# Splitting the matmuls of an accumulated output into two of half the columns, in a channel-attention and feed-forward kernel

## The chip, the cores and the metric

The kernel runs on one core of a Trainium2 chip. The metric is the device time of one execution in microseconds (us), the median of several runs.

## What is computed

Two batches of 6016 tokens with 256 channels go through an attention over channels, and the result through a feed-forward layer with 2048 hidden units. The reference, cut:

```python
def _attn_ref(q, k, v, tau):               # B, N, C = 2, 6016, 256
    qn = q / (np.linalg.norm(q, axis=1, keepdims=True) + 1e-06)
    kn = k / (np.linalg.norm(k, axis=1, keepdims=True) + 1e-06)
    s = kn.transpose(0, 2, 1) @ qn / tau
    ...
    return (v @ a).astype(np.float32)      # a: softmax of s

def _moe_ref(x, w_in, w_out):              # 12032 tokens, 256 -> 2048 -> 256
    h = x @ w_in
    g = h * (1.0 / (1.0 + np.exp(-h)))
    return (g @ w_out).astype(np.float32)
```

## The kernel before, in words

The first part (about 121 us) loads q and k, forms the 256 x 256 scores of the first batch on TensorE in float32 (L244), turns them into the attention matrix, and decodes the two weight matrices. `mix` (L361) multiplies the attention into w_in, so that what is left is two large products: w_in mixed with the attention, by v; and w_out, by the activated hidden units.

The tokens go by in 12 "pairs" (L386): five of 1024 tokens and one of 896 for each batch. A pair is two halves of `h` tokens, h = 512 or 448, and `h` is the number of columns of every large matmul. For each pair there are eight steps `i`, one for each 256 hidden units. `emit_pair_group` (L499) makes the hidden units of one step in seven products of a Strassen-Winograd scheme (`product`, L507), each of three float16 matmuls (L509) that add up in a PSUM bank; ScalarE and VectorE copy, add and apply SiLU (L516, L521, L525), and `finish` splits each tile of 128 hidden units by `h` tokens into a float16 high and low part, `hl` (`split`, L123 on ScalarE and L124 on VectorE).

`emit_out` (L467) takes one such tile and adds its share to the output: for each of the two blocks `e` of 128 output channels, three matmuls (L480) of `h` columns, of w_out's low part by hl's high part, high by low, and high by high. They add up in a PSUM bank `o` over all 16 tiles (NF) of one half of a pair, so a bank gets 48 matmuls. Every matmul has a weight load of its own before it. When the count `c` reaches 16, ScalarE (L489) and VectorE (L493) scale the two banks into `sb`, and SP's queue writes it out (L497).

The order of TensorE's work is that of the program text: `emit_pair_group` yields four times a step, and at each yield at most one pending tile (two in parts of the first pair) goes through `emit_out`; background work (the next pair's v, the second batch's attention) is queued behind markers. TensorE executes its instructions in order, but for weight loads, which are drawn ahead of matmuls.

Of the kernel before, what the change touches and what calls it, by code (L numbers as in the profile page):

```python
# [16 lines left out]
P = 128  # L17
#: Operands of the large products are scaled by powers of two to at most 2**TOP.
TOP = 13
#: The hidden activations are scaled down by 2**-GS: 256 products of at most 2**(2 * TOP).  # L20
GS = 2 * TOP + 8 - 15
# [3 lines left out]
def channel_attention_then_silu_ffn(ctx, tc, q, k, qT, kT, vT, tau, w_in, w_out, outT):  # L25
# [34 lines left out]
    def small_psum(name):  # L60
        """Before the first output accumulates, its banks are free."""
        if early[0]:
            return ps_o.tile([P, 512], F32, tag="o", name=name)
        return ps_b.tile([P, 512], F32, tag="z", name=name)

    @contextmanager
    def at(priority):
        """Instructions of lower number go first where several could."""
        was = tc.cur_priority
        tc.cur_priority = priority  # L70
        yield
        tc.cur_priority = was

    def pow2_scale(amax, tag, bufs=1):
        """amax: largest magnitude by partition. Returns (s, 1/s): a power of two with
        |x| s < 2**TOP. Yields where TensorE waits for VectorE."""
        pt = small_psum("pt")
        nc.tensor.transpose(pt[:1, :P], amax, ident)
        mx = sm.tile([1, 1], F32, tag="mx", name="mx")
        nc.vector.tensor_reduce(out=mx, in_=pt[:1, :P], op=ALU.max, axis=AX.X)  # L80
        yield
        pb = small_psum("pb")
        nc.tensor.matmul(pb[:, :1], ones[:1, :], mx, start=True, stop=True)
        bound = sm.tile([P, 1], F32, tag="bound", name="bound")
        nc.vector.tensor_scalar(
            out=bound, in0=pb[:, :1], scalar1=2.0**-40, scalar2=2.0**40, op0=ALU.max, op1=ALU.min
        )
        yield
        floor2 = sm.tile([P, 1], F32, tag="floor2", name="floor2")
        nc.vector.tensor_scalar(  # L90
            out=floor2.bitcast(U32), in0=bound.bitcast(U32), scalar1=0x7F800000, scalar2=None,
            op0=ALU.bitwise_and,
        )
        inv = sm.tile([P, 1], F32, tag=f"i{tag}", name=f"i{tag}", bufs=bufs)
        nc.vector.tensor_scalar(
            out=inv, in0=floor2, scalar1=2.0 ** (1 - TOP), scalar2=None, op0=ALU.mult
        )
        s = sm.tile([P, 1], F32, tag=f"s{tag}", name=f"s{tag}", bufs=bufs)
        nc.vector.reciprocal(s, inv)
        yield  # L100
        return s, inv

    def amax_of(parts, tag):
        """Largest magnitude by partition over the tiles."""
        m = sm.tile([P, len(parts)], F32, tag=tag, name=tag)
        for i, x in enumerate(parts):
            nc.vector.tensor_reduce(
                out=m[:, i : i + 1], in_=x, op=ALU.max, axis=AX.XY if len(x.shape) == 3 else AX.X,
                apply_absolute_value=True,
            )  # L110
            yield
        r = sm.tile([P, 1], F32, tag=f"{tag}1", name=f"{tag}1")
        nc.vector.tensor_reduce(out=r, in_=m, op=ALU.max, axis=AX.X)
        yield
        return r

    def split(src, hi, lo, s=None):
        """hi + lo = src * s."""
        if s is None:
# [14 lines left out]
    def decode(dst, raw, top=None):  # L134
        """dst <- float32 of the float64 in raw (as 64 raw bits). Yields after each step.
        top: takes the largest high word by partition, without sign."""
        k, n = raw.shape[1:]
        w = raw.bitcast(U32).rearrange("p k (n two) -> p k n two", two=2)
        low, high = w[:, :, :, 0], w[:, :, :, 1]
        t = hp.tile([P, k, n], U32, tag="g", name="t", bufs=6)  # L140
        # What float32 has no exponent for becomes 0.
        nc.scalar.activation(out=t.bitcast(F32), in_=high.bitcast(F32), func=AF.Abs)
# [29 lines left out]
    def warm(func, x):  # L172
        """Has func's table loaded while ScalarE waits."""
        nc.scalar.activation(out=junk, in_=x, func=func)

    # -- channel attention ---------------------------------------------------------------
    # Tokens that come at a time; the first ones sooner.
    edges = [0, *range(2, J, G), J], [*range(0, J, G), J]
# [18 lines left out]
    def square_sums():  # L197
        """Squares of the last batch's q and k, summed along the tokens. Yields."""
        edges = list(range(0, N, NT)) + [N]
# [15 lines left out]
    def attention(b, ahead):  # L215
        """Yields after each piece of TensorE's work."""
        if b == 0:
# [32 lines left out]
        while b and "go" not in norms:  # L250
            yield
        # Squared norms by partition.
        tot = sm.tile([P, 2 * KC], F32, tag="tot", name="tot", bufs=1)
# [21 lines left out]
        yield  # L275
        # One step of Heron's rule makes the root exact to float32.
        rn = sm.tile([P, 2 * KC], F32, tag="rn", name="rn", bufs=1)
# [56 lines left out]
        yield  # L334
        # The softmax's denominators scale the rows of a's product with w_in.
        rows = sm.tile([P, KC], F32, tag="rows", name="rows")
# [10 lines left out]

    # Left operands of the seven products of Strassen and Winograd. Rows 1 and 2 of the pair's
    # product are its odd and its even block of hidden units.
    A21, A11, A22, A12, S1, S2, S3, S4 = range(8)  # L350
    # Right operands. The columns are the halves of the tokens.
    B11, T1, B21, B22, T2, T3, T4 = range(7)
    mixed = {}

    def mix(b, i):
        """w_in's hidden units of pair i, mixed by the attention, in parts."""
        aT, rows = mixer[b]
# [26 lines left out]

    # -- tokens --------------------------------------------------------------------------
    pairs = [(b, n, min(NT, N - n)) for b in range(B) for n in range(0, N, NT)]  # L386
# [57 lines left out]
    def back_of(p):  # L444
        """What takes the accumulated output of pair p back to its scale."""
        back = sm.tile([P, 1], F32, tag="back", name="back")
        nc.vector.reciprocal(back, parts[p][2])
        nc.vector.tensor_scalar(
            out=back, in0=back, scalar1=weights["out"][1], scalar2=None, op0=ALU.mult
        )  # L450
        return back
# [6 lines left out]
    def finish(t):  # L458
        """hi and lo of a tile of hidden activations."""
        h = t["h"]  # L460
# [6 lines left out]
    def emit_out(t):  # L467
# [6 lines left out]
        for e in range(KC):  # L474
# [4 lines left out]
            for i, (a, m) in enumerate(((wo_lo, 0), (wo_hi, 1), (wo_hi, 0))):  # L479
                nc.tensor.matmul(  # L480
                    o[:, :h], a[:, f, ee], hl[:, m, :h],
                    start=(c == 1 and i == 0), stop=(c == NF and i == 2),
                )
        if c == NF:
# [14 lines left out]
    def emit_pair_group(p, i):  # L499
        """Hidden units of pair i for the tokens of pair p. Yields where other work of TensorE  # L500
        may stand, four times."""
        b, n, w = pairs[p]
# [55 lines left out]
    def steps(gen):  # L558
        """Runs gen to its end; its value."""
        while True:  # L560
            try:
                next(gen)
            except StopIteration as e:
                return e.value
# [14 lines left out]
    def prepare_out():  # L579
        """w_out in parts; its raw halves stand where later tokens will."""  # L580
        halves = [vp.tile([P, NI, C], F32, tag="v", name="wo", bufs=3) for _ in range(2)]
# [29 lines left out]
    def high_to_f32(x):  # L611
        """In place: from the high word of positive float64 to float32, its mantissa cut."""
        t = sm.tile([P, 1], U32, tag="hw", name="hw", bufs=1)
# [40 lines left out]

    # Priorities, by phase.
    VALUES, RAW, CHAIN, DECODE, MAIN = 20000, 15000, 10000, 25000, 100000
    # The groups of tokens behind which w_in's parts are loaded.
    RAW_AT = (4, 5, 6, 7, 8, 9, 9, 9)

    with at(0):  # L660
# [3 lines left out]
        nc.vector.reciprocal(rtau, tau_sb)  # L664
        # Both norms come doubled.
        nc.vector.tensor_scalar(out=rtau, in0=rtau, scalar1=4.0, scalar2=None, op0=ALU.mult)
# [21 lines left out]
    def mark():  # L688
        """What background() traces next goes behind what was traced by now."""
        found = {}  # L690
# [4 lines left out]
    def background(gen, n=1):  # L695
        """Next steps of gen, issued no sooner than what mark() saw last."""
        start = len(traced())
# [54 lines left out]
    def prepare():  # L752
        """Next steps of w_out's preparation, and of the other batch's attention."""
        nonlocal filler
# [100 lines left out]
```

## Time and profile before

| | |
|---|---|
| three runs | 1067.05, 1069.79, 1070.09 us; median 1069.79 us |
| span of the profiled execution, first to last instruction | 1063.3 us (its own time isn't given beside it) |
| TensorE matmuls | 1040.3 us, 98% of the span, 4886 |
| TensorE weight loads | 523.7 us, 49%, 4886 |
| VectorE | 728.5 us, 69% |
| ScalarE | 837.3 us, 79% |
| mean granted TensorE clock | 1.000 |

Between the span and the median of the runs lie 6.5 us. Busy time is the union of an engine's records. A matmul's record (379 ns for 512 columns) is longer than the distance to the next one, because matmuls are pipelined: what a matmul costs is read from the distance of starts, not from its mean duration.

### The profile page before, as it was taken

Reading aid. Unit: us, or ns where it says so; the run is one execution under the profiler, and the core shown is the slowest. Engines: PE = TensorE matmul, PEld = TensorE weight load, DVE = VectorE, ACT = ScalarE, POOL = GpSimd, SP = SyncE. Lnnn points to the kernel's source line nnn. Section 1 sums busy time; section 2 is a strip of 40 time slices with the busy share of each in tenths; the row PEclk is TensorE's granted clock in tenths of the full one; section 3 lists DMA queues with packets and bytes.
Section 4 is the critical chain, followed back from the end, with each engine's and each line's share of the span. In section 5 each row is a group of like instructions: output and inputs, shape, how many; then the busy total and the mean of one; then the engine's idle time right before and its main releaser. Section 6 shows DMA issues by size and latency. Waiting matters only on the chain.

```text
span 1063.3 us, 13048 instructions
## 1 busy us (share of the span) xinstructions
PE 1040.3 (98%) x4886; PEld 523.7 (49%) x4886; DVE 728.5 (69%) x1288; ACT 837.3 (79%) x1371; POOL 0.7 (0%) x6
## 2 busy tenths in 40 slices
PE   7889999999999999999999999999999999999998
PEld 6667544444444444444555544444444444444554
DVE  6989669657657657667768767657657657656654
ACT  5657568889989989988878878878878878878875
POOL 0000000000000000000000000000000000000000
PEclk9999999999999999999999999999999999999999
DMA  8978711111412400200200200200200100100100
GB/s 317 343 261 288 270 42 40 60 60 58 133 39 60 137 1 1 80 0 1 80 1 1 75 1 1 79 1 1 75 1 1 40 1 1 40 1 1 40 1 35
DMA packets 25391, 70.83 MB, mean 67 GB/s; under 512 B 2544, under 2 KB 3824, under 8 KB 25328
## 3 DMA queue, kind: packets, MB, share of 16 engines
q1 hardware_dynamic: 25328, 70.00, 18.9%
q8 instruction: 38, 0.62, 0.2%
q14 instruction: 25, 0.20, 0.1%
HBM read 57.67 MB, written 12.32 MB: 66 GB/s over the span
## 4 chain that ended last, share of the span: by engine, by line
PE 81%; ACT 8%; DVE 6%; DMA 4%; issue 1%; SPq 0%; DVEq 0%
PE o L480 40%; PE x L509 20%; PE y L509 10%; PE z L509 5%; PE sc L244 3%; ACT g L525 2%; ACT hl L123 2%; PE w L361 2%; DMA q_t<-in_q 2%; DVE g L521 1%; ACT c L516 1%; DVE hl L124 1%; DMA raw<-in_w_out 1%; DMA held<-in_w_in 1%; DMA raw<-in_w_in 1%
## 5 line engine op out<-in xcount | busy, mean ns | idle before, releaser
L480 PE MATMUL o<-hl,wo_hi 128*128 128x512 f16 (+1 forms) x1536 | 450.5, 375 | 0.0
L124 DVE SCALAR_TENSOR_TENSOR hl<-g,sg,hl 128x512 f16<-128x512 f32 (+1 forms) x384 | 282.5, 739 | 175.1 <-ACT hl L123 173.5
L509 PEld LDWEIGHTS <-W 128*128 128x128 f16 x2016 | 196.1, 98 | 228.4 <-issue 5.7
L509 PE MATMUL x<-m,W 128*128 128x512 f16 (+1 forms) x1152 | 306.4, 374 | 1.5 <-DVE g L521 0.9
L525 ACT ACTIVATE g<-g,alpha 128x512 f32<-128x512 f32 (+1 forms) x288 | 203.7, 707 | 117.0 <-DVE g L521 115.5
L480 PE MATMUL o<-hl,wo_lo 128*128 128x512 f16 (+1 forms) x768 | 287.5, 375 | 0.0
L123 ACT ACTIVATE hl<-g,sg 128x512 f16<-128x512 f32 (+1 forms) x384 | 271.5, 711 | 10.1
L480 PEld LDWEIGHTS <-wo_hi 128*128 128x128 f16 x1536 | 150.3, 98 | 173.4
L509 PE MATMUL y<-m,W 128*128 128x512 f16 (+1 forms) x576 | 153.2, 375 | 0.0
L516 ACT COPY c<-x 128x512 f32<-128x512 f32 (+1 forms) x192 | 110.5, 576 | 25.1 <-PE x L509 22.4
L480 PEld LDWEIGHTS <-wo_lo 128*128 128x128 f16 x768 | 75.1, 98 | 86.9
L244 PE MATMUL sc<-q_t,k_t 128*128 128x256 f32 x376 | 88.2, 387 | 13.5 <-DMA q_t<-in_q 13.3
L521 DVE TENSOR_TENSOR g<-z,c 128x512 f32<-128x512 f32 (+1 forms) x96 | 65.2, 680 | 40.8 <-PE z L509 33.8
L521 DVE TENSOR_TENSOR g<-x,c 128x512 f32<-128x512 f32 (+1 forms) x96 | 65.2, 679 | 40.9 <-PE x L509 40.6
L244 PEld LDWEIGHTS sc<-q_t,k_t 128*128 128x128 f32 x376 | 71.1, 193 | 27.3 <-issue 9.4
L521 DVE TENSOR_TENSOR g<-y,c 128x512 f32<-128x512 f32 (+1 forms) x96 | 65.0, 677 | 26.3 <-ACT c L516 25.4
L509 PE MATMUL z<-m,W 128*128 128x512 f16 (+1 forms) x288 | 76.5, 375 | 0.0
L516 ACT COPY c<-y 128x512 f32<-128x512 f32 (+1 forms) x96 | 54.7, 570 | 11.9 <-PE y L509 10.7
L525 ACT ACTIVATE g<-x,alpha 128x512 f32<-128x512 f32 (+1 forms) x96 | 63.4, 660 | 0.8 <-PE x L509 0.8
L124 DVE SCALAR_TENSOR_TENSOR m<-v_t,sv,m 128x512 f16<-128x512 f32 (+1 forms) x48 | 35.0, 735 | 0.1
L123 ACT ACTIVATE m<-v_t,sv 128x512 f16<-128x512 f32 (+1 forms) x48 | 33.7, 708 | 0.0
L124 DVE SCALAR_TENSOR_TENSOR m<-x,sv,m 128x512 f16<-128x512 f32 (+1 forms) x36 | 26.4, 737 | 9.3 <-ACT m L123 9.3
(111 smaller groups left out, 467.3 us busy)
## 6 DMA issues: line engine op xcount, KB each, us to landing
k_t<-in_k SPq DMA_DIRECT2D x22, 512.0 KB, 5.8
q_t<-in_q SPq DMA_DIRECT2D x22, 512.0 KB, 5.9
v_t<-in_vT SPq DMA_DIRECT2D x10, 1024.0 KB, 5.1
outT<-sb SPq DMA_DIRECT2D x40, 256.0 KB, 2.0
turned<-in_qT SPq DMA_DIRECT2D x10, 512.0 KB, 4.4
turned<-in_kT SPq DMA_DIRECT2D x10, 512.0 KB, 3.5
raw<-in_w_out SPq DMA_DIRECT2D x8, 512.0 KB, 4.3
raw<-in_w_in SPq DMA_DIRECT2D x5, 512.0 KB, 6.9
```

Of the source, the lines that this page charges most:

```text
L123: nc.scalar.activation(out=hi, in_=src, func=AF.Copy, scale=s)
L124: nc.vector.scalar_tensor_tensor(out=lo, in0=src, scalar=s, in1=hi, op0=ALU.mult, op1=ALU.subtract)
L244: nc.tensor.matmul(sc[:, cb, :], t["k"][:, i, cb * P : (cb + 1) * P], t["q"][:, i, :], start=(j + i == 0 and cb == 0), stop=(j + i == J - ...
L361: nc.tensor.matmul(w[:, cb * C : (cb + 1) * C], aT[:, db, cb * P : (cb + 1) * P], w_in_sb[:, db, i * C : (i + 1) * C], start=(cb + db == 0 ...
L480: nc.tensor.matmul(o[:, :h], a[:, f, ee], hl[:, m, :h], start=(c == 1 and i == 0), stop=(c == NF and i == 2),)
L509: nc.tensor.matmul(bank[:, :h], wm[:, u, a - 1], m[:, y, x, :h], start=(first and j == 0), stop=(j == 2), skip_group_check=True,)
L516: nc.scalar.copy(t[:, :h], bank[:, :h])
L521: nc.vector.tensor_tensor(out=g[:, :h], in0=bank[:, :h], in1=t[:, :h], op=ALU.add)
L525: nc.scalar.activation(out=g[:, :h], in_=src[:, :h], func=AF.Silu, scale=alpha)
```

## The change

In `emit_out`, each of the three matmuls of a block is issued as two, over the first and the second half of the columns (256 and 256, or 224 and 224), both with the same left operand, so that each has a weight load apiece. The start flag, which marks a bank as to be overwritten, is kept for the first half of the first matmul alone; the second half of the bank is overwritten too, since nothing has been written there since. The rest of the diff takes comments and docstrings out, lines for lines, and changes nothing that is executed.

```diff
             for i, (a, m) in enumerate(((wo_lo, 0), (wo_hi, 1), (wo_hi, 0))):
-                nc.tensor.matmul(
-                    o[:, :h], a[:, f, ee], hl[:, m, :h],
-                    start=(c == 1 and i == 0), stop=(c == NF and i == 2),
-                )
+                for u in range(0, h, h // 2):
+                    nc.tensor.matmul(
+                        o[:, u : u + h // 2], a[:, f, ee], hl[:, m, u : u + h // 2],
+                        start=(c == 1 and i == 0 and u == 0), stop=(c == NF and i == 2),
+                        skip_group_check=True,
+                    )
```

## Rows read from the trace of the kernel before

**Rows 1.** The page's first two parts: busy time, share of the span and instructions of each engine; the granted TensorE clock in 40 slices, in tenths, 9 being 90% or more.

```profile
PE 1040.3 (98%) x4886; PEld 523.7 (49%) x4886; DVE 728.5 (69%) x1288; ACT 837.3 (79%) x1371; POOL 0.7 (0%) x6
...
PEclk9999999999999999999999999999999999999999
```

**Rows 2.** The page's fourth part: the chain of work that ended last, shares of the span by engine, then by line.

```profile
PE 81%; ACT 8%; DVE 6%; DMA 4%; issue 1%; SPq 0%; DVEq 0%
PE o L480 40%; PE x L509 20%; PE y L509 10%; PE z L509 5%; PE sc L244 3%; ACT g L525 2%; ACT hl L123 2%; PE w L361 2%; DMA q_t<-in_q 2%; DVE g L521 1%; ACT c L516 1%; DVE hl L124 1%; DMA raw<-in_w_out 1%; DMA held<-in_w_in 1%; DMA raw<-in_w_in 1%
```

**Rows 3.** Busy time by windows: the stretch, its length, then for each engine busy us and (x) the count, the granted clock, the DMA share and GB/s.

```profile
121.00:200.00 79.00, 78.25 (x357) 38.30 (x356) 61.29 (x120) 60.54 (x105) 0.00 (x0) 1.00 0.21 73
200.00:440.00 240.00, 240.00 (x1115) 109.06 (x1114) 159.34 (x258) 212.95 (x347) 0.00 (x0) 1.00 0.20 65
440.00:600.00 160.00, 158.86 (x781) 81.35 (x779) 113.06 (x217) 132.88 (x228) 0.00 (x0) 1.00 0.08 27
600.00:1000.00 400.00, 400.00 (x1864) 182.86 (x1862) 267.51 (x433) 318.26 (x503) 0.00 (x0) 1.00 0.06 21
1000.00:1063.30 63.30, 58.66 (x311) 30.14 (x308) 31.72 (x49) 44.93 (x74) 0.00 (x0) 0.99 0.04 15
```

**Rows 4.** Groups of instructions with shapes kept apart: the matmuls of L480 (count, busy us, mean ns of a record).

```profile
L480 PE MATMUL o<-hl,wo_hi 128*128 128x512 f16 x1280 | 381.2, 379 | 0.0
...
L480 PE MATMUL o<-hl,wo_lo 128*128 128x512 f16 x640 | 242.4, 379 | 0.0
L480 PE MATMUL o<-hl,wo_hi 128*128 128x448 f16 x256 | 69.3, 352 | 0.0
...
L480 PE MATMUL o<-hl,wo_lo 128*128 128x448 f16 x128 | 45.1, 352 | 0.0
```

**Rows 5.** Two stretches without a pause, TensorE alone, by windows (length, busy us, count, clock, DMA share, GB/s): in the first every matmul has 512 columns, in the second 448. Each window begins inside the record of the first counted matmul and ends just before the next one after the last counted starts.

```profile
640.53:679.85 39.32, 39.32 (x183) 1.00 0.08 27
1000.45:1049.41 48.96, 48.96 (x260) 1.00 0.00 1
```

**Rows 6.** The timeline of TensorE's matmuls (start us, us): the first matmul counted in the first stretch of rows 5 and the one that follows its last, then the same of the second stretch (the first of the two that the row merges).

```profile
640.36 0.38 PE L480 MATMUL o<-hl,wo_lo 128*128 128x512 f16 x1
...
679.86 0.38 PE L509 MATMUL x<-m,W 128*128 128x512 f16 x1
...
1000.24 0.54 PE L480 MATMUL o<-hl,wo_hi 128*128 128x448 f16 x2
...
1049.42 0.35 PE L480 MATMUL o<-hl,wo_lo 128*128 128x448 f16 x1
```

**Rows 7.** The line L480 by itself: duration of its weight loads and matmuls, minimum/median/maximum in ns, with the forms.

```profile
L480 PEld LDWEIGHTS <-wo_hi x1536: 96/98/100, 121.4 to 1058.1; 128*128 128x128 f16 x192
...
L480 PEld LDWEIGHTS <-wo_lo x768: 96/98/98, 121.2 to 1057.7; 128*128 128x128 f16 x192
```

**Rows 8.** The chain of work in order of time: start us, us, what. Two pieces in which TensorE's stream itself is the chain.

```profile
121.54 1.29 PE o L480 x6
122.84 1.73 PE w L361 x8
```

**Rows 9.** The timeline around 63.3 us: three matmuls of 128 float32 columns in a row (two of L323, one of L78), the one after them, and their weight loads.

```profile
63.27 0.38 PE L323 MATMUL tp<-ident,e 128*128 128x128 f32 x2
63.48 0.27 PE L78 MATMUL pt<-ident,wtop 128*1 128x128 f32 x1
63.59 0.38 PE L244 MATMUL sc<-q_t,k_t 128*128 128x256 f32 x1
...
63.17 0.24 PEld L323 LDWEIGHTS tp<-ident,e 128*128 128x128 f32 x2
63.38 0.08 PEld L78 LDWEIGHTS pt<-ident,wtop 128*1 128x1 f32 x1
```

**Rows 10.** The timeline around 448 us, seen through narrow windows: the last three of four matmuls of 128 float32 columns (L291), the L480 matmul after them, and that one's weight load with the last of L291's before it.

```profile
447.88 0.50 PE L291 MATMUL rq_ps<-diag,ones 128*128 128x128 f32 x3
448.00 0.19 PEld L291 LDWEIGHTS rq_ps<-diag,ones 128*128 128x128 f32 x1
448.11 0.10 PEld L480 LDWEIGHTS <-wo_hi 128*128 128x128 f16 x1
...
448.22 0.38 PE L480 MATMUL o<-hl,wo_hi 128*128 128x512 f16 x1
```

**Rows 11.** The timeline around 949.6 us, seen through two narrow windows: the weight loads of L509 after a pause, first one, then the first two together.

```profile
949.59 0.10 PEld L509 LDWEIGHTS <-W 128*128 128x128 f16 x1
...
949.59 0.11 PEld L509 LDWEIGHTS <-W 128*128 128x128 f16 x2
```

**Rows 12.** The timeline around 20.9 us, where TensorE's sequencer had nothing queued: a weight load after a wait, and the matmul behind it; [idle before it, and what ended that].

```profile
20.84 0.08 PEld L78 LDWEIGHTS pt<-ident,av 128*1 128x1 f32 x1 [1.01 <-issue]
20.87 0.27 PE L78 MATMUL pt<-ident,av 128*1 128x128 f32 x1 [0.64 <-DVE av L113]
```

**Rows 13.** DMA queues, kind: packets, MB, share of 16 engines; the queue of instruction fetches that goes with TensorE's count.

```profile
q8 instruction: 38, 0.62, 0.2%
```

**Rows 14.** Waits of TensorE from 121 us on: who waited for whom, us in total, times, longest us.

```profile
PEld L509 <- issue: 5.1, 16, 0.9
PEld pb L83 <- DVE g L521: 3.8, 9, 0.4
...
PE x L509 <- DVE g L521: 0.9, 2, 0.6
```

## The prediction

> **What bounds the kernel now.** I read the page's busy times first, then the chain, then the busy times by stage. TensorE is busy for 98% of the span and its granted clock is full, the 2.4 GHz level, in all slices [rows 1]. That alone proves little, since a matmul's record is longer than the time it takes in a stream. The chain says more: 81% of it is TensorE, and half of that is the line that the change splits, L480 [rows 2]. By stage it is plainer still: from 200 to 440 us and from 600 to 1000 us TensorE shows no idle time at all, in 440 to 600 us 1.1 us, in 121 to 200 us 0.8 us, and the 4.6 us of the last window are the way of the last output to memory [rows 3]. ScalarE is the next engine, at 89% of the stretch from 200 to 440 us (212.95 of 240) and at 80% of the one from 600 to 1000 us. So what TensorE's stream gains or loses behind 121 us arrives at the end nearly one for one. L480 has no part in the first 121 us.
>
> **What one matmul of the stream costs.** Its distance to the next one, which two stretches without a pause give, one for each width. With 512 columns: 183 matmuls in 679.86 - 640.36 = 39.50 us, 215.8 ns each. With 448: 260 in 1049.42 - 1000.24 = 49.18 us, 189.2 ns [rows 5, 6]. 64 columns are worth 26.7 ns, 0.417 ns a column, one cycle at 2.4 GHz. At that price 512 columns take 213.3 ns and 448 take 186.7, so 2.5 ns of each distance belong to the matmul whatever its width. Each of these matmuls had a weight load of its own, so a load is in the price already.
>
> **The change, part by part.**
>
> Matmuls: L480 has 1280 + 640 of 512 columns and 256 + 128 of 448, 2304 in all [rows 4]. Each becomes two, with the same columns in sum. Columns cost what they did; the fixed part comes once more: 2304 x 2.5 ns = 5.8 us. By the stream's price a half of 256 columns takes 106.7 + 2.5 = 109.2 ns.
>
> Weight loads: 2304 more. One takes 98 ns by its record [rows 7], and today it lies beside a matmul of 216 ns. Is 109 ns cover enough? The trace has no matmul of 256 float16 columns, so I bound it by two nearby cases of about 107 ns of streaming (128 float32 columns; eight records of 256 float32 columns take 1.73 us in the stream, 216 ns each, six of 512 float16 columns 1.29, 215 ns: a float32 column costs two cycles) [rows 8]. Around 63.3 us three such matmuls, each behind a load, start at 63.27 and end their turn at 63.59: 107 ns each [rows 9]. Around 448 us three start at 447.88 and the next one of L480 at 448.22: 113 ns each, with loads of 190 ns, and the last of the three distances had a 100 ns load of L480 in it [rows 10]. The low end is thus nothing beyond the fixed part, the high end 113 - 109.2 = 3.8 ns for each of 4608 halves, 17.5 us more. I take the low end, because what stretches the second case is the length of a float32 load: after a pause two float16 loads follow each other within some 10 to 20 ns (the record of one is 0.10 us, of two together 0.11) [rows 11], so nearly all of the 98 ns is latency that overlaps.
>
> Issue: twice as many instructions for the same time, two each 109 ns. Where the sequencer had nothing queued, a matmul follows its load after 30 ns (20.84, 20.87) [rows 12]: 60 ns for a pair, under 109. Code: 38 fetches brought some 9,800 instructions of TensorE, 16 KB each [rows 13]; 4608 more instructions need 18 more fetches, against stretches of 240 and 400 us in which the present ones left no idle time [rows 3]. Taken as nothing; without that cover a fetch would have to show as a pause, and none does.
>
> What hides a little of it: TensorE waits now and then for a tile from VectorE or ScalarE, in all 1.9 us of plain idle time from 121 to 600 us [rows 3], with the waits of single loads listed one by one [rows 14]. A longer stretch of L480 ahead of such a wait shortens it. At most these 1.9 us come back, at least none; I take 0.6 us, a third, since most waits for L83 hang on TensorE's own earlier work. No wait, DMA or buffer is added: a bank's readers come after its last matmul, as before. ScalarE and VectorE get 0.5% more time for the same work.
>
> Sum: 5.8 - 0.6 = +5.2 us. On the profiled execution that is a span of 1063.3 + 5.2 = 1068.5 us; the 6.5 us between span and median stay. 1069.8 + 5.2 = 1075.0 us, 0.5% slower. A measurement of this kernel can tell about 0.3%, 3.2 us, from no change.
>
> **The rivals.**
>
> Not slower. The fixed 2.5 ns belong to the exchange of one set of weights for another, not to a matmul; the second half brings the set that is there already (or its load is dropped), follows without a gap, and the sum is 0, or -0.6 with the shorter waits: 1069 to 1070 us. It decides if the second half starts 106.7 ns behind the first and not 109. Against it: the price is the same wherever it can be read, behind 98 ns loads and behind one of 84 ns with a single column [rows 9]. For it: no row shows the same weights twice in a row. To be faster by 3.2 us it would also have to remove more idle time than the 1.9 us there are.
>
> Loads that don't fit. Halves at 113 ns, as around 448 us [rows 10]: 5.8 + 17.5 = 23.3 us, 1093 us; in part, at 111 ns, some 14 us, 1084 us. Against it, the 10 to 20 ns between two loads [rows 11].
>
> Issue-bound. If an instruction in a long stream took the sequencer twice the 30 ns, 60 ns, a pair would take 120 ns: 4608 x 10.8 = 50 us more, 1126 us. Against it, the two instructions 30 ns apart with nothing queued ahead of them [rows 12]. The Trainium skill's page "TensorE: Matmul & The Clock Gate" (Part 1, "Wait — 56ns, not 53.3ns?") allows for this case: it puts a matmul at about 62 ns where the sequencer's firmware decodes it, which with as much for a load would make 1144 us. The trace disagrees, with half of that for an instruction.
>
> Serial loads. If a load could not lie beside a matmul that uses the whole array, 2304 more would cost 98 ns each, 226 us: 1301 us. The same page says so (Part 3, "What overlaps and what doesn't": loads overlap matmuls in flight only in other row groups). The trace disagrees: 216 ns a matmul leave no room for a serial 98 ns beside 213 ns of columns [rows 5, 7].
>
> **How the numbers follow.** Chances: the forecast 0.74; not slower 0.10; loads that don't fit 0.12; issue-bound 0.03; serial loads 0.01. The likeliest gives 1075.0 us. The range: low end 1070.0, which is the "not slower" case at its top, and also the forecast if the runs land as low as the fastest one shown (1067.05) with part of the waits returned; high end 1089, between the partly and the wholly exposed load. Left out are most of the issue-bound and serial cases, the far end of the loads, and the lower half of "not slower": about 0.15 together. Slower by over 0.3%: 0.66 of the forecast's 0.74 (the rest falls within, by scatter) + 0.12 + 0.03 + 0.01 = 0.82. Within 0.3%: 0.08 + 0.07 = 0.15. Faster: 0.03.
>
> **What would show it.** 7190 matmuls and as many loads, 4608 on L480; L480's halves 109 ns apart and the 224-column ones 96; a block that was six matmuls, 1.29 us [rows 8], at 1.31; no pause of TensorE where a fetch lands. Halves 111 to 113 ns apart show the load, 120 the sequencer, 106.7 within a pair the "not slower" case. I am wrong if the order of TensorE's instructions around L480 has changed, or if idle time appears where there is none now.

## The result, and the profile after

The changed kernel took 1073.80 us, the median of 12 runs (1071.62 to 1079.82); the kernel before 1066.55 us, the median of 12 (1064.80 to 1070.09). The ratio is 1.0071, 95% interval 1.0054 to 1.0089: slower by 7.6 us, 5.8 to 9.5. The forecast was slower by 5.2 us, just below that interval.

The page of the changed kernel: busy time, share and count of each engine; the granted clock in tenths; the queue of instruction fetches; the chain that ended last, by line. They answer to [rows 1, 2, 13].

```profile
PE 1046.6 (98%) x7190; PEld 746.8 (70%) x7190; DVE 730.2 (68%) x1288; ACT 840.1 (79%) x1371; POOL 0.7 (0%) x6
...
PEclk9999999999999999999999999999999999999999
...
q8 instruction: 56, 0.92, 0.3%
...
PE o L481 41%; PE x L511 20%; PE y L511 11%; PE z L511 5%; PE sc L244 3%; DMA q_t<-in_q 2%; ACT g L527 2%; PE w L361 2%; ACT hl L123 1%; DMA k_t<-in_k 1%; DVE g L523 1%; ACT c L518 1%; DVE hl L124 1%; ACT m L123 1%; DMA raw<-in_w_out 1%; DMA held<-in_w_in 1%
```

7190 matmuls and loads, 18 more fetches, as counted ahead. (L480 is L481 now, and the lines of the products and adds are two further down.) What one tile (two blocks `e`) costs stands in the chain of work in order of time (start us, us, what), from a stretch without a pause:

```profile
642.16 1.31 PE o L481 x12
643.47 0.65 PE x L511 x3
```

Twelve halves in 1.31 us are 109.2 ns each, where six whole matmuls took 1.29 us [rows 8]: the halves cost the 2.5 ns apiece and nothing else. 2304 x 2.5 ns = 5.8 us, and 1.8 us of the difference are still to be found. Busy time by windows, with the columns of [rows 3] and to be held against them:

```profile
121.00:200.00 79.00, 78.02 (x524) 54.28 (x523) 60.81 (x120) 59.97 (x103) 0.00 (x0) 1.00 0.20 67
200.00:440.00 240.00, 240.00 (x1696) 165.67 (x1694) 159.51 (x258) 211.80 (x343) 0.00 (x0) 1.00 0.20 65
440.00:600.00 160.00, 157.63 (x1145) 115.09 (x1144) 110.79 (x214) 132.56 (x227) 0.00 (x0) 1.00 0.08 27
600.00:1000.00 400.00, 400.00 (x2824) 277.35 (x2822) 266.72 (x431) 317.60 (x500) 0.00 (x0) 1.00 0.05 19
```

TensorE's plain idle time from 440 to 600 us is 2.4 us, and was 1.1; from 121 to 200 us it is 1.0, and was 0.8. It is idle for longer than before, though VectorE and ScalarE, whose tiles it waits for, have the same work and slightly more time for it.

Whole runs of one kernel spread by 5 to 8 us, more than what is sought, so I read the traces over the main stretch: from the start of the first matmul of the output to the end of the last one, each from its row in the timeline (start us, us). For the changed kernel 1065.34 - 120.26 = 945.08 us:

```profile
120.26 0.38 PE L481 MATMUL o<-hl,wo_lo 128*128 128x256 f16 x2
...
1064.79 0.55 PE L481 MATMUL o<-hl,wo_hi 128*128 128x224 f16 x4
```

Beside it I give TensorE's waits in that stretch. Each matmul's start is held against the median distance behind matmuls of the same width and type (216, 189, 109, 96 ns and so on); where it comes over 10 ns later, what is over the median counts, summed over the stretch.

### The profile page after: what moved, and what is told of

Read it like the earlier page. It is cut to its first block, busy times and chain, and to the rows that moved or that the text cites. A ratio compares the mean times of both kernels' runs of the same rounds, so it can differ in the third digit from the quotient of the medians.

```text
span 1069.9 us, 17658 instructions
## 1 busy us (share of the span) xinstructions
PE 1046.6 (98%) x7190; PEld 746.8 (70%) x7190; DVE 730.2 (68%) x1288; ACT 840.1 (79%) x1371; POOL 0.7 (0%) x6
## 4 chain that ended last, share of the span: by engine, by line
PE 82%; ACT 7%; DVE 5%; DMA 5%; issue 1%; SPq 0%; DVEq 0%; ACTq 0%
PE o L481 41%; PE x L511 20%; PE y L511 11%; PE z L511 5%; PE sc L244 3%; DMA q_t<-in_q 2%; ACT g L527 2%; PE w L361 2%; ACT hl L123 1%; DMA k_t<-in_k 1%; DVE g L523 1%; ACT c L518 1%; DVE hl L124 1%; ACT m L123 1%; DMA raw<-in_w_out 1%; DMA held<-in_w_in 1%
## 5 line engine op out<-in xcount | busy, mean ns | idle before, releaser
L481 PE MATMUL o<-hl,wo_hi 128*128 128x256 f16 (+1 forms) x3072 | 455.5, 270 | 0.0
L481 PEld LDWEIGHTS <-wo_hi 128*128 128x128 f16 x3072 | 299.8, 98 | 30.5
L481 PE MATMUL o<-hl,wo_lo 128*128 128x256 f16 (+1 forms) x1536 | 290.1, 270 | 0.0
L481 PEld LDWEIGHTS <-wo_lo 128*128 128x128 f16 x1536 | 150.1, 98 | 91.0
```

The costliest lines, as they stand in the source:

```text
L481: nc.tensor.matmul(o[:, u : u + h // 2], a[:, f, ee], hl[:, m, u : u + h // 2], start=(c == 1 and i == 0 and u == 0), stop=(c == NF and i ...
```

## The experiments

All main stretches and waits, worked out as above from one trace each (two each of the kernel before and the changed one show how well they repeat):

| kernel | main stretch, us | against before | TensorE's waits, us | stretch less waits, us | ratio of times (95%) |
|---|---|---|---|---|---|
| before (first trace, again) | 937.28, 937.48 | 0 | 6.4, 6.5 | 930.9, 931.0 | again: 1.0001 (0.9987 to 1.0015) |
| changed (first trace, again) | 945.08, 944.92 | +7.7, +7.5 | 8.4, 8.2 | 936.7, 936.7 | 1.0071 (1.0054 to 1.0089), 1.0064 (1.0044 to 1.0083) |
| split, old order | 942.26 | +4.9 | 5.6 | 936.7 | 1.0060 (1.0040 to 1.0079) |
| new order, no split | 940.91 | +3.5 | 10.0 | 930.9 | 1.0031 (1.0020 to 1.0043) |
| new order of TensorE alone | 938.59 | +1.2 | 7.7 | 930.9 | 1.0003 (0.9983 to 1.0024) |
| new order of ScalarE and VectorE alone | 940.05 | +2.7 | 9.2 | 930.9 | 1.0019 (1.0007 to 1.0031) |
| split, halves outermost, old order | 942.37 | +5.0 | 5.7 | 936.7 | 1.0060 (1.0035 to 1.0084) |
| quarters, old order | 953.32 | +15.9 | 5.1 | 948.2 | 1.0159 (1.0136 to 1.0181) |
| uneven split, old order | 942.78 | +5.4 | 6.1 | 936.7 | 1.0049 (1.0033 to 1.0064) |
| products split, old order | 941.65 | +4.3 | 5.8 | 935.8 | 1.0063 (1.0045 to 1.0080) |

Without its waits the stretch is 931 us in every kernel with whole matmuls, whatever the order, and 936.7 in every one with L480 in two pieces: 5.8 us.

**Where the other 1.8 us come from.** The order of the instructions on each engine is made by a planner, which moves instructions out of the order of the text. The part ahead gives TensorE's order as that of the text; in the kernel before, 290 of its 4616 places are filled otherwise. With other matmuls the planner made another order. Laid side by side, with the halves of a matmul taken as one, 113 of TensorE's 4616 places, 76 of ScalarE's 1336 and 52 of VectorE's 1280 are filled differently; SP's queue is the same. Theory: the new order costs the rest. Rival: it belongs to the doubled instructions. So I held each engine to a written order, with the split and without:

```diff
+    for name, engine in (("PE", E.PE), ("Activation", E.Activation), ("DVE", E.DVE)):
...
+        order = [i for u, w in ORDER[name] for unit in units[u:w] for i in unit]
+        for x, y in zip(order, order[1:]):
+            tc.add_manual_dep(
+                y, x.name,
...
```

`units` are the engine's instructions in the order of the text (both halves of a matmul as one unit), and `ORDER` the places of the order wanted, of before or of the changed kernel. Such a dependency is of the kind without a semaphore (`NoSync`, behind the dots). The traces of ScalarE and VectorE have the orders that were asked for: those of before in the split with the old order, those of the changed kernel in the one without the split.

> The split, with TensorE, ScalarE and VectorE held to the order of the kernel before (the changed kernel's planner gave ScalarE 76, VectorE 52 and TensorE 113 places another order). Theory: 2304 more matmuls cost 2.5 ns each, 5.8 us, and what the changed kernel lost beyond that is the new order, whose waits of TensorE are longer: with the old order +5.0 to +5.8 us, ratio 1.0047 to 1.0055, and TensorE's waits from 440 to 600 us no longer than before (1.1 us plain idle). Rival: the order doesn't matter and the rest belongs to the doubled instructions: the ratio stays where the changed kernel's is, 1.007.

> No split, but the order of instructions that the planner gave the changed kernel. Theory: the order costs TensorE some 1.5 to 2 us more waiting, ratio 1.0015 to 1.002, with plain idle of TensorE from 440 to 600 us at 2.4 us instead of 1.1. Rival (the order is free): 1.000, with the idle time of before.

> The kernel before against itself. Every theory: ratio 1.000, to within 0.0015. The granted clock of its executions is of interest: those of the changed kernel had 0.996 to 1.000. If the kernel before has the same spread, the clock is no part of the difference; if it is at 1.000 throughout, up to 2 us of the difference are the clock's.

> The changed kernel again, beside the others on one chip. Theory: the sum of the two runs before this one, 5.0 to 5.8 us of the split plus 1.5 to 2 us of the order: ratio 1.0065 to 1.0072. Rival (the order is free, the first result was high by scatter): 1.005.

The four ran on one chip. The split in the old order has TensorE's waits at 5.6 us, 0.9 us under before's (6.4 and 6.5), and a main stretch 4.9 us longer: 5.8 - 0.9. Its ratio of times, 1.0060, is over the expected 1.0047 to 1.0055, and against the changed kernel's 1.0064 it does not stand apart; by whole runs alone, the old order is not shown to win anything. Six runs are few for that, and its profiled run began slowly (first output matmul at 126.93 us, granted clock 0.97 in the first 121 us). Its windows (as above) show the idle time back at before's level from 440 to 600 us, 0.85 us; the second row is the same window with the new order and no split, 2.55 us:

```profile
440.00:600.00 160.00, 159.15 (x1156) 116.21 (x1155) 111.08 (x218) 133.35 (x225) 0.00 (x0) 1.00 0.07 25
```

```profile
440.00:600.00 160.00, 157.45 (x774) 79.80 (x773) 111.32 (x215) 133.09 (x227) 0.00 (x0) 1.00 0.08 27
```

The order alone makes the unsplit kernel slower, ratio 1.0031, its interval clear of 1, main stretch +3.5 us with 3.6 us more waits. I had expected 1.5 to 2 us: in the changed kernel the longer stretches of L480 take part of these waits back (10.0 to 8.4 and 8.2 us). So the parts add up: order +3.5, matmuls +5.8, waits returned -1.7, together +7.6, beside +7.7 and +7.5 measured. In part that is bookkeeping, since a stretch is distances plus waits; what it shows is that nothing else is left. The kernel before against itself stays at 1.0001, and the granted clock of its runs has the same spread as that of the changed kernel's (0.996 to 1.000); in both it is 1.00 in all windows from 121 to 1000 us. These runs show no part of the clock in the difference.

What stays open is the time outside the main stretch. Against the kernel before, the medians of whole runs differ by 0.3 to 2.0 us more than the main stretch in the five kernels with pieces and the old order, and by 0.2 to 1.3 us less in those with a new order. Whether that is the scatter of the loading stage can't be told from one or two traces a kernel. The +3.5 us of the order are borne out by time; the 2.7 us between the changed kernel and the split in the old order stand in the main stretch of the traces alone.

One such exchange can be seen in the trace. VectorE at the step to the second batch, first the kernel before (its second trace), then the changed one, and TensorE's wait in each (start us, us; [idle before, and what ended it]):

```profile
590.06 0.61 DVE L521 TENSOR_TENSOR g<-x,c 128x448 f32<-128x448 f32 x1
590.59 0.68 DVE L425 TENSOR_TENSOR x<-v_t,x 128x512 f32<-128x512 f32 x1
...
590.72 0.73 PE L509 MATMUL x<-m,W 128*128 128x448 f16 x3 [0.60 <-DVE g L521]
```

```profile
592.12 0.69 DVE L425 TENSOR_TENSOR x<-v_t,x 128x512 f32<-128x512 f32 x1
592.72 0.62 DVE L523 TENSOR_TENSOR g<-x,c 128x448 f32<-128x448 f32 x1
...
593.39 0.54 PE L511 MATMUL x<-m,W 128*128 128x448 f16 x2 [0.96 <-DVE g L523]
```

In the changed kernel the next pair's preparation (L425) goes ahead of the add that frees bank `x` for TensorE's next product, and TensorE is idle for 0.96 us instead of 0.60.

**Whose order.** Two kernels without the split, with one half of the new order each.

> No split; TensorE alone has the order that the planner gave the changed kernel, ScalarE and VectorE have theirs of before. The order of all three cost 3.5 us between the first matmul of the output and TensorE's last. Theory: TensorE's order, which has other places only from about 150 to 200 us, makes under 1 us of it, and the rest is ScalarE's and VectorE's order, which puts work for the next pair ahead of tiles that TensorE waits for. Rival: it is TensorE's order, 2.5 us or more.

> The counterpart: ScalarE and VectorE in the order of the changed kernel, TensorE in that of before, no split. Theory: 2.5 us or more of the 3.5. Rival: under 1 us.

Main stretch +1.2 us and +2.7 us, waits the same. As expected, the larger part is ScalarE's and VectorE's; TensorE's is a little more than the 1 us allowed, and its order differs not only early, as expected: 31 of the 113 places lie in the second third of its instructions. By time, the first is no difference that can be measured, the second 1.0019 with its interval clear of 1. A kernel held to the order that its planner gave anyway was not run. If the parts add, holding an order costs some 0.4 us by itself (an estimate: 1.2 + 2.7 less the 3.5 of both together).

**What a matmul and its load really cost.** The halves left a load 109 ns of cover, more than its 98. To see whether that was luck, L480's matmuls were cut finer, in the old order (the edits are against the split; the slices below these lines change with them):

```diff
-                for u in range(0, h, h // 2):
+                for u in range(0, h, h // 4):
```

> L480's matmuls in four of 128 (112) columns, 9216 with a load each, in the order of the kernel before. If the fixed part alone counts (53.3 + 2.5 = 55.8 ns): 3 x 2304 x 2.5 = 17.3 us more, 1084 us. If the next load can't be hidden behind less than its own 98 ns: 9216 x 98 = 903 us in place of the present 487, 1482 us. If the sequencer's 30 ns an instruction bind, 60 ns a pair: 66 us more, 1132 us. The theory is the first, with the loads' hiding as the step in doubt: 128 columns leave 56 ns.

```diff
-                for u in range(0, h, h // 2):
+                for u, w in ((0, h - 64), (h - 64, 64)):
```

> The split into h - 64 and 64 columns, order of the kernel before: as many instructions and columns as in the changed kernel, but the load behind the short piece has 26.7 + 2.5 = 29 ns of cover. If a load needs no cover of its own: +5 us as with the halves. If a pair has a floor by the sequencer of 60 ns: 2304 x 31 = 71 us more than that, 1142 us. If the load's whole 98 ns has to pass behind the short piece's start: 2304 x 69 = 159 us more, 1230 us.

The quarters took 1083.25 us, ratio 1.0159, where the fixed part alone gave 1084. The chain in order of time, one tile of the quarters, then one of the uneven split:

```profile
641.57 1.34 PE o L482 x24
```

```profile
641.00 1.31 PE o L482 x12
```

24 quarters of 128 columns in 1.34 us are 55.8 ns each; six pairs of 448 and 64 columns in 1.31 us are 218 ns a pair, as for the halves. A load is hidden behind 56 ns and even behind the 28 ns that pass from the start of a piece of 64 columns to the next one's: the loads overlap one another. In the timeline of the weight loads of the uneven split, a row that merges two of them lasts 0.13 us, while one by itself lasts 0.10:

```profile
641.46 0.13 PEld L482 LDWEIGHTS <-wo_lo 128*128 128x128 f16 x2
641.68 0.10 PEld L482 LDWEIGHTS <-wo_hi 128*128 128x128 f16 x1
```

The last output of the quarters bounds the sequencer (start us, us), with 120 quarters of 112 columns in a row:

```profile
1074.83 0.36 PE L482 MATMUL o<-hl,wo_lo 128*128 128x112 f16 x4
...
1080.33 0.56 PE L482 MATMUL o<-hl,wo_hi 128*128 128x112 f16 x8
```

From the first to the start of the last eight, 112 matmuls with a load each took 5.50 us: a load and a matmul every 49 ns, without a pause. In the uneven split a piece of 448 columns stands 190 ns ahead of the next matmul and one of 64 columns 28 ns, where the price by width gives 189 and 29; why the two differ is open, but the pair costs what two halves cost, and the stretch without waits is that of the halves, 936.7 us.

**Whether the same weights matter.** The halves of a matmul bring the same weights twice. In the split, four of the six matmuls of a block `e` come behind one with the same weights, since `wo_hi` is used twice; with the halves outermost only two of six do, all else as in the split with the old order:

```diff
-            for i, (a, m) in enumerate(((wo_lo, 0), (wo_hi, 1), (wo_hi, 0))):
-                for u in range(0, h, h // 2):
+            for u in range(0, h, h // 2):
+                for i, (a, m) in enumerate(((wo_lo, 0), (wo_hi, 1), (wo_hi, 0))):
```

> The split with the order of the six matmuls of a block changed: all three of the first half, then all three of the second, so that no matmul has the weights of the one before it; everything else in the order of the kernel before. Theory (the 2.5 ns belong to a matmul, whatever weights it brings): the same as the split in that order, TensorE's main stretch +5.0 us. Rival (weights that are there already cost less): more than that, up to 5.8 us more.

Main stretch 942.37 us against 942.26, ratio 1.0060 for both: no difference. The expectation is wrong in that some weights still stand twice in a row, but 1536 more changes of weights at 2.5 ns would have been 3.8 us.

The kernel before could have told as much: the second and third matmul of its blocks share `wo_hi`. Two of them together last 0.54 us where one lasts 0.35 [rows 6], so they start 0.19 us apart, the full 189 ns of 448 columns. Over its trace, for 512 columns and leaving out the matmuls that wait, the distance to a second one with the same weights is 215.8 ns, and 215.9 where the weights change.

**Whether it is L480.** Its matmuls are whole again, and those of the products (L509) are halved:

```diff
-                nc.tensor.matmul(
-                    bank[:, :h], wm[:, u, a - 1], m[:, y, x, :h],
-                    start=(first and j == 0), stop=(j == 2), skip_group_check=True,
-                )
+                for v in range(0, h, h // 2):
+                    nc.tensor.matmul(
+                        bank[:, v : v + h // 2], wm[:, u, a - 1], m[:, y, x, v : v + h // 2],
+                        start=(first and j == 0 and v == 0), stop=(j == 2), skip_group_check=True,
+                    )
```

> L480 whole as before; the 2016 matmuls of the seven products (L509) are the ones issued as two halves, in the order of the kernel before. Theory: 2016 x 2.5 = 5.0 us on TensorE, less up to 1 us by shorter waits: main stretch +4.0 to 5.0 us, ratio 1.004 to 1.005. Rival (the cost belongs to long sums in one bank, or to L480): under 2 us or over 8 us.

Main stretch +4.3 us: 4.9 for the matmuls less 0.6 us of shorter waits. L509's matmuls cost what L480's do. The ratio of times, 1.0063, is over the expected 1.004 to 1.005; its interval begins at 1.0045, 4.8 us, half a microsecond over what the main stretch shows.

## Why the prediction was right in direction, and short in size

- **TensorE's stream sets the end.** Right: from 200 to 440 and from 600 to 1000 us it still has no idle time, and in all ten experiments the medians of whole runs follow the main stretch to within 2 us.
- **The fixed part, 2.5 ns for a matmul, read from two widths [rows 5, 6].** Right, for 256 and 128 columns and for a pair of 448 and 64 too: 5.8 us for the halves, 17.3 for the quarters.
- **Loads hidden, issue and fetches free.** Right. For the low end between 107 and 113 ns the prediction gave that float16 loads follow each other closely [rows 11], and the quarters bear that out. That the length of float32 loads makes the 113 ns [rows 10] was argued and is not shown: the last of those three distances, with the 100 ns load in it, is 112 ns in the trace. The 30 ns for an instruction [rows 12] were too careful: load and matmul together pass in 49.
- **Waits returned, 0.6 us, and the order as before.** This is the step that failed. The prediction took the order of instructions as given, added no wait, and said that it would be wrong if the order had changed; it had. With the order held, waits did shrink, by 0.9 us (taken: 0.6; the bound was 1.9), and the split cost 4.9 us in the main stretch against the 5.2 forecast. The new order put 3.5 us of waits on the other side, of which the split's longer stretches returned 1.7.
- **Sum.** +5.2 us forecast, +7.6 by time, interval 5.8 to 9.5. That the time forecast, 1075.0 us, is so near the measured 1073.8 is luck: its base was 3.2 us too high (1069.79 from three runs, 1066.55 from twelve), which made up for a change that was put too small.
- **Rivals.** "Not slower" falls twice over: halves with the same weights stand 109 ns apart, and changing weights more often costs no more. The prediction held that no row shows the same weights twice in a row; the kernel before does, at the full price, so the trace at hand already spoke against this rival. "Loads that don't fit" falls by the halves at 109.2 ns, and it, "issue-bound" and "serial loads" fall by the quarters at 55.8 ns, less than one load's record. The page "TensorE: Matmul & The Clock Gate" of the Trainium skill puts a matmul at 62 ns where firmware decodes it (Part 1, "Wait — 56ns, not 53.3ns?"). That price does not apply here, where load and matmul together pass in 49 to 56 ns. The Trainium skill's same page lets a load overlap matmuls in flight only in other row groups (Part 3, "What overlaps and what doesn't"). The traces disagree: loads of 98 ns for the whole array fit behind whole-array matmuls 55.8 ns apart. The formula that the Trainium skill's same page gives for one matmul by itself, columns at 2.4 GHz plus 2.5 ns (Part 2, "Back-to-back issue gap"), holds here with a load for every matmul, at 215.8, 109.2 and 55.8 ns.

## What to carry to other kernels

In a stream without pauses, read a matmul's price from the distance of starts at two widths: the slope is the columns, the rest is what each further matmul costs, and it is small, with the weight load inside it. Where a planner orders the instructions, an edit's price is its own cost plus that of the new order; compare the order on each engine before a residue is put down to the hardware, and hold the order fixed to tell the two apart. When the differences are a few microseconds, compare the stretch of the trace that the edit touches, since the loading stage's scatter is as large.

## What was not expected of the hardware

That the weight load's 98 ns would fit into the 28 ns of a matmul of 64 columns: two consecutive loads' records together last 0.13 us. That the same weights twice in a row cost as much as new ones. And that the loading stage would scatter so much by itself: the first matmul of the output starts anywhere from 120.26 to 127.57 us in these traces, with the same instructions ahead of it. In the trace of the split with the old order, where it starts at 126.93 us, the granted clock averaged 0.97 over the first 121 us; in that of the uneven split it starts at 124.44 us with the clock at 1.00.
